# First x tiles in two loads, tile 0's key products ahead of tile 1's transposes, w1 in one load

## The chip, the cores and the metric

The kernel runs on one core of a Trainium2 chip. A core has TensorE (PE, with its weight loads listed apart as PEld), VectorE (DVE), ScalarE (ACT), GpSimd (POOL) and SyncE (SP), which here only issues DMAs. Each engine takes its instructions in order and waits on semaphores of the others. DMA transfers run on 16 DMA engines that all queues share. The metric is the device time of one execution in microseconds; before, the median of 4 runs is 178.98 us (178.72 to 179.65).

## The reference

x is [2048, 512] in bf16. A linear attention with 32 heads of 16 and a gated MLP with 1376 hidden columns work on the same x, and a gate per token mixes them:

```
g   = sigmoid((x * gate_w).sum(-1))
q, k, v = split(x @ wqkv)                      # 32 heads of 16
phi(t) = where(t > 0, t + 1, exp(t)) + 1e-6
kv  = phi(k)^T v   per head;  z = sum over tokens of phi(k)
a   = (phi(q) kv) / (phi(q) z + 1e-6) @ wo
b   = (silu(x @ w1) * (x @ w3)) @ w2
out = g * a + (1 - g) * b
```

## The kernel before

Tokens are worked in 16 tiles of 128 (index `t`) and 4 blocks of 512 (`tb`). All weights are loaded once into SBUF and stay. x is held twice: `x_sb`, tokens on partitions, and `xT`, features on partitions in four chunks `kc`.

**Loads (lines 78 to 111).** All but one are issued by SP, in the order of the code; ACT issues the first half of `wk_sb` (line 83). The first load brings x tiles 0 and 1 in one transfer, `x_first`: partition p gets rows 2p and 2p+1, 2 KB in one piece, so that tile 0 holds the even rows of the first 256 and tile 1 the odd ones. Their results are stored by the same rule (`out_first`, line 376). `xT` of tiles 2 and 3 comes by a DMA transpose from memory (line 87), that of the blocks 1 to 3 by three more (line 91), between which x tiles 2 to 15 are loaded (line 96). Then come wq, the remainder columns `wr_sb` with the gate's weights, wv, halves of w1 and w3 in turn (lines 105 to 107), wo, w2.

**The front (lines 153 to 181, 382 to 391).** TensorE's order is the order of the code (a manual schedule). It begins with nine matmuls on constants that nothing uses, `emit_warm` (line 165): six of 512 columns, three of 128. Then `xT` of tiles 0 and 1 is made by TensorE: `emit_xT(t)` does four 128x128 transposes into two PSUM buffers; VectorE copies the first two chunks to `xT` (line 179), ScalarE the other two (line 181). Then come the key products `emit_k_mm(k_ps, t, kc)` (line 184), 128x512 each, of tiles 0 to 3. Their first eight are in the order (kc, t) = (0,0), (1,0), (0,1), (1,1), (2,0), (3,0), and then chunks 2 and 3 of tile 1. Products of chunks 0 and 1 read the half of `wk_sb` that ACT loads, those of chunks 2 and 3 the half that SP loads (line 84). `emit_k_phi` (lines 138 to 148) turns a finished k into phi(k): exp on ScalarE (140), two operations on VectorE (142, 145), and a running sum on GpSimd.

**The rest.** For t from 4 on, `emit_xp` (line 204: x^T phi(k), in four PSUM banks through all tiles) of an earlier tile and `emit_k(t)` alternate. After that come q of block 0, the remainder columns, z, the product with wv, and W = kv wo folded. Then for each block the MLP's chunks `emit_ffn` (gate products line 312, up products line 320) and the output tiles `emit_out` (lines 353 to 362), with the next block's q between them. The last output tile is stored in three parts.

Of the kernel before, what the change touches and what calls it, by code (L numbers as in the profile page):

```python
# [17 lines left out]
def kernel(  # L18
# [13 lines left out]
    P = nc.NUM_PARTITIONS  # L32
# [7 lines left out]
    TB = 512  # L40
# [4 lines left out]
    FM = FC * P  # L45
# [3 lines left out]
    x2d = A_x.flatten_outer_dims()  # L49
    out2d = out.flatten_outer_dims()  # L50
# [11 lines left out]
    x_sb = consts.tile([P, NT, D], BF16, name="x_sb")  # L62
# [4 lines left out]
    w1_sb = consts.tile([P, KC, FM], BF16, name="w1_sb")  # L67
# [7 lines left out]
    w1_r = B_w1.rearrange("(kc d) f -> d kc f", d=P)  # L75
    w3_r = B_w3.rearrange("(kc d) f -> d kc f", d=P)
    x_r = x2d.rearrange("(t p) d -> p t d", p=P)
    dq = nc.sync
    TF = 2
    x_first = x2d[0 : TF * P, :].rearrange("(p j) d -> p j d", j=TF)  # L80
    out_first = out2d[0 : TF * P, :].rearrange("(p j) d -> j p d", j=TF)
    dq.dma_start(out=x_sb[:, 0:TF, :], in_=x_first)
    nc.scalar.dma_start(out=wk_sb[:, 0:2, :], in_=wqkv_r[:, 0:2, D : 2 * D])
    dq.dma_start(out=wk_sb[:, 2:4, :], in_=wqkv_r[:, 2:4, D : 2 * D])
    pre = consts.tile([1, 1], FP32, name="pre")
# [2 lines left out]
        out=xT[:, :, TF * P : TB], in_=x2d[TF * P : TB, :], transpose=True  # L88
    )
    for tb in range(1, NTB):  # L90
        dq.dma_start(
            out=xT[:, :, tb * TB : (tb + 1) * TB], in_=x2d[tb * TB : (tb + 1) * TB, :],
# [7 lines left out]
    with nc.allow_non_contiguous_dma(reason="one gate weight per partition and chunk"):  # L100
        dq.dma_start(
            out=wr_sb[:, :, 2 * FR : NR], in_=gate_w.rearrange("(kc d o) -> d kc o", d=P, o=1)
        )
    dq.dma_start(out=wv_sb[:], in_=wqkv_r[:, :, 2 * D : 3 * D])
    for fsl in (slice(0, FM // 2), slice(FM // 2, FM)):
        dq.dma_start(out=w1_sb[:, :, fsl], in_=w1_r[:, :, fsl])
        dq.dma_start(out=w3_sb[:, :, fsl], in_=w3_r[:, :, fsl])
    dq.dma_start(out=wo_sb[:], in_=A_wo.rearrange("(kc d) n -> d kc n", d=P))
    w2_r = B_w2[0:FM, :].rearrange("(fc f) d -> f fc d", f=P)
# [9 lines left out]
        out=bm, in_=bm, pattern=[[-Dh, HPC], [0, Dh]], compare_op=ALU.is_ge, fill=0.0,  # L119
# [3 lines left out]
        out=bm, in_=bm, pattern=[[Dh, HPC], [0, Dh]], compare_op=ALU.is_ge, fill=0.0,  # L123
# [34 lines left out]
    def emit_warm(*widths):  # L158
        warm = psX.tile([P, TB], FP32, tag="XP3", name="warm")
        for n in widths:  # L160
            nc.tensor.matmul(
                warm[:, 0:n], lhsT=warm_l, rhs=warm_r[:, 0:n], start=True, stop=True
            )

    emit_warm(TB, TB, TB, TB, TB, TB, P, P, P)

    st = {}

    def emit_xT(t):
        for h in range(2):  # L170
            xTp = psX.tile([P, 2, P], BF16, tag=f"XP{(2 * t + h) % 4}", name="xTp")
            for j in range(2):
                kc = 2 * h + j
                nc.tensor.transpose(  # L174
                    out=xTp[:, j, :], in_=x_sb[:, t, kc * P : (kc + 1) * P], identity=ident[:]
                )
            xT_t = xT[:, 2 * h : 2 * h + 2, t * P : (t + 1) * P]
            if h == 0:
                nc.vector.tensor_copy(out=xT_t, in_=xTp[:])  # L179
            else:  # L180
                nc.scalar.activation(out=xT_t, in_=xTp[:], func=ACT.Copy)

    def emit_k_mm(k_ps, t, kc):
        nc.tensor.matmul(  # L184
            k_ps[:], lhsT=xT[:, kc, t * P : (t + 1) * P], rhs=wk_sb[:, kc, :],
            start=(kc == 0), stop=(kc == KC - 1),
        )
# [148 lines left out]
    def emit_out(tb, tt):  # L336
        t = tb * TPB + tt
        tsl = slice(tt * P, (tt + 1) * P)

        if t < NT - 1:  # L340
            parts = [(0, D, True)]
        else:
            h, q7 = D // 2, 7 * D // 8
            parts = [(0, h, True), (h, q7, True), (q7, D, True)]
        if t < NT - 1:
            o_out = work.tile([P, D], BF16, tag="o_out", name="o_out")
        else:
            o_out = consts.tile([P, D], BF16, name="o_last")
        lo = 0
        for i, (a, b, store) in enumerate(parts):  # L350
            o_ps = psX.tile([P, b - a], FP32, tag=f"XP{2 + (tt + i) % 2}", name="o_ps")
            for c in range(KC):
                nc.tensor.matmul(  # L353
                    o_ps[:], lhsT=st[tb, "pqT"][:, c, tsl], rhs=W_sb[:, c, a:b],
                    start=(c == 0), stop=False,
                )
            nc.tensor.matmul(  # L357
                o_ps[:], lhsT=st[tb, "hTr"][:, tsl], rhs=w2r_sb[:, a:b],
                start=False, stop=False,
            )  # L360
            for fc in range(FC):
                nc.tensor.matmul(  # L362
                    o_ps[:], lhsT=st[tb, "hT"][:, fc, tsl], rhs=w2_sb[:, fc, a:b],
                    start=False, stop=(fc == FC - 1),
                )
            if i < 2:
                nc.scalar.activation(  # L367
                    out=o_out[:, a:b], in_=o_ps[:], func=ACT.Copy, scale=omg[:, t : t + 1]
                )
            else:  # L370
                nc.vector.tensor_scalar(
                    out=o_out[:, a:b], in0=o_ps[:], scalar1=omg[:, t : t + 1], scalar2=None,
                    op0=ALU.mult,
                )
            if store:
                rows = out_first[t] if t < TF else out2d[t * P : (t + 1) * P, :]
                eng = nc.scalar if i == 1 else nc.sync
                eng.dma_start(out=rows[:, lo:b], in_=o_out[:, lo:b])
                lo = b


    k0 = [psM.tile([P, D], FP32, tag="mm", name=f"k0_{t}") for t in range(TPB)]
    emit_xT(0)
    emit_xT(1)
    for kc, t in ((0, 0), (1, 0), (0, 1), (1, 1), (2, 0), (3, 0)):
        emit_k_mm(k0[t], t, kc)
    emit_k_phi(k0[0], 0)
    for t in range(1, TPB):
# [15 lines left out]
    with tc.manual_schedule(engines={ENG.DVE}):  # L404
# [18 lines left out]
        for dc in range(KC):  # L423
# [9 lines left out]
            out=z_sb[:].rearrange("p (b f) -> p b f", f=Q),  # L433
            in_=z_col[:, :, None].to_broadcast([P, NB, Q]),
        )
        kvT_ps = psX.tile([P, KC, P], FP32, tag="XP0", name="kvT_ps")
        for c in range(KC):
# [7 lines left out]
            out=kvT_sb[:], in0=kvT_ps[:],  # L445
# [22 lines left out]
    for tb in range(NTB):  # L468
        for fc in range(FC if tb == 0 else 0, FC):
            emit_ffn(tb, fc)  # L470
        nx = tb + 1
        for tt in range(TPB):
            if nx < NTB:
                emit_q(nx, tt, psX, "XP0")
                if tt % 2 == 0:
                    emit_rem(nx, tt // 2, psX, "XP1")
                    if tt == 2:
                        emit_omg(nx)
            emit_out(tb, tt)
            if nx < NTB:  # L480
                emit_den(nx, tt)
        if nx < NTB:
            emit_norm(nx)
# [30 lines left out]
```

## Time and profile before

| | |
|---|---|
| median of 4 runs | 178.98 us (178.72 to 179.65) |
| the profiled execution's own time | 178.82 us |
| its span, first to last instruction | 177.1 us |
| TensorE busy | 172.4 us, 97% |
| VectorE busy | 118.6 us, 67% |
| ScalarE, GpSimd busy | 65.4 and 63.9 us |
| DMA moved | 15.14 MB, mean 85 GB/s |

A row of the groups or of the timeline gives the line of the kernel, the engine, the operation and its tiles (out<-in). In the timeline the first two columns are start and length in us; the bracket at the end is idle time before it and what ended that. In the chain of waits the columns are start, length and what the time was spent in. Matmuls are pipelined, so a row of one matmul (379 ns) is longer than the step to the next. PEld rows mark when a matmul's weights are loaded, which is when its wait for data shows.

### The profile page before, as it was taken

The page shows a single profiled execution, that of the slowest core. Times are in us where ns is not written, and L with a number is a line of the kernel's source. Part 1 is how long each engine was busy: PE and PEld are TensorE (multiplying, and loading weights), DVE is VectorE, ACT ScalarE, POOL GpSimd, SP SyncE. Part 2 cuts the span into 40 slices and gives each one's busy share as a digit, 9 for nine tenths or more (in the row PEclk, how much of TensorE's full clock was granted, in tenths as well). Part 3 has the DMA queues.
Part 4 walks back from the last instruction along what each step waited for, and adds up shares of the span by engine and source line. Part 5 has one row for each costly group of instructions (what it writes and reads, how often), then busy time and mean ns, then how long its engine had stood idle before and what let it go on. Part 6 is the DMA issues. An engine that isn't in the chain of part 4 may idle for free.

```text
span 177.1 us, 2457 instructions
## 1 busy us (share of the span) xinstructions
PE 172.4 (97%) x867; PEld 83.4 (47%) x883; DVE 118.6 (67%) x204; ACT 65.4 (37%) x123; POOL 63.9 (36%) x80
## 2 busy tenths in 40 slices
PE   7999999999999999999999999999999999999993
PEld 3444444474445454444454544444545444444463
DVE  0586858899999637597876466978754668776000
ACT  3624224465433333334244333233434323241221
POOL 6197655789062323272003232710032328000000
PEclk9999999999999999999999999999999999999999
DMA  5999989941013011123000101230002022200012
GB/s 171 233 288 222 256 291 364 352 145 28 9 30 89 7 41 37 37 59 89 0 4 7 48 26 43 73 71 6 0 7 67 7 70 59 59 0 0 30 38 54
DMA packets 30380, 15.14 MB, mean 85 GB/s; under 512 B 20928, under 2 KB 30240, under 8 KB 30368
## 3 DMA queue, kind: packets, MB, share of 16 engines
q1 hardware_dynamic: 29952, 14.67, 30.5%
q10 hardware_dynamic: 416, 0.31, 0.5%
q8 instruction: 7, 0.11, 0.3%
q14 instruction: 5, 0.04, 0.1%
HBM read 8.42 MB, written 2.10 MB: 59 GB/s over the span
## 4 chain that ended last, share of the span: by engine, by line
PE 96%; DMA 2%; issue 1%; DVE 0%
PE o_ps L362 19%; PE gate_ps L312 19%; PE up_ps L320 19%; PE o_ps L353 8%; PE XP L204 8%; PE q_ps L217 8%; PE k_ps L184 6%; PE r_ps L241 3%; PE k L184 2%; PE o_ps L357 2%; DMA x_sb<-in_A_x_dram 2%; PE kvT_ps L440 1%; PE W_ps L458 0%; DVE xT L179 0%; PE xTp L174 0%
## 5 line engine op out<-in xcount | busy, mean ns | idle before, releaser
L312 PE MATMUL gate_ps<-xT,w_sb 128*128 128x512 bf16 x157 | 40.7, 379 | 0.2
L320 PE MATMUL up_ps<-xT,w_sb 128*128 128x512 bf16 x157 | 40.7, 379 | 0.2
L225 POOL TENSOR_TENSOR qz<-pq,z_sb 128x512 f32<-128x512 bf16 x16 | 18.5, 1164 | 58.0 <-DVE pq L145 58.0
L325 ACT ACTIVATE th<-gate_ps 128x512 bf16<-128x512 f32 x40 | 23.9, 597 | 39.0 <-PE gate_ps L312 37.5
L362 PE MATMUL o_ps<-w_sb,hT 128*128 128x512 bf16 (+3 forms) x177 | 37.3, 355 | 0.2
L327 DVE SCALAR_TENSOR_TENSOR gs<-th,gate_ps 128x512 bf16<-128x512 bf16 x40 | 27.3, 682 | 5.4 <-ACT th L325 5.1
L332 DVE TENSOR_TENSOR hT<-up_ps,gs 128x512 bf16<-128x512 f32 x40 | 27.6, 691 | 3.8
L142 DVE TENSOR_SCALAR phi_m<-phi_e 128x512 bf16<-128x512 bf16 x32 | 13.6, 425 | 21.1 <-ACT phi_e L140 20.9
L362 PEld LDWEIGHTS <-hT 128*128 128x128 bf16 x180 | 16.9, 98 | 17.8
L320 PEld LDWEIGHTS <-w_sb 128*128 128x128 bf16 x160 | 15.7, 98 | 18.9
L312 PEld LDWEIGHTS <-w_sb 128*128 128x128 bf16 x160 | 15.6, 98 | 18.6
L292 POOL TENSOR_TENSOR pqn<-pq,rden 128x512 bf16<-128x512 bf16 x16 | 16.6, 1057 | 15.1 <-DVE rden L285 13.1
L367 ACT ACTIVATE o_out<-o_ps,omg 128x512 bf16<-128x512 f32 x15 | 10.3, 688 | 28.9 <-PE o_ps L362 28.9
L194 POOL TENSOR_TENSOR pks<-pks,pk_sb 128x512 f32<-128x512 f32 x15 | 17.5, 1170 | 7.3 <-DVE pk_sb L145 6.7
L353 PE MATMUL o_ps<-W_sb,pqT 128*128 128x512 bf16 (+3 forms) x70 | 16.7, 355 | 0.1
L204 PE MATMUL XP<-pk_sb,x_sb 128*128 128x512 bf16 x62 | 16.2, 379 | 0.1
L228 DVE TENSOR_REDUCE den<-qz 128x32 f32<-128x512 f32 x16 | 10.9, 684 | 7.9 <-POOL qz L225 7.9
L217 PE MATMUL q_ps<-wq_sb,xT 128*128 128x512 bf16 x61 | 16.1, 379 | 0.1
L140 ACT ACTIVATE phi_e<-k_ps 128x512 bf16<-128x512 f32 x12 | 7.2, 597 | 14.4 <-PE k_ps L184 14.4
L140 ACT ACTIVATE phi_e<-q_ps 128x512 bf16<-128x512 f32 x16 | 9.6, 597 | 7.8 <-PE q_ps L217 6.7
L184 PE MATMUL k_ps<-wk_sb,xT 128*128 128x512 bf16 x48 | 12.3, 379 | 0.0
L145 DVE SCALAR_TENSOR_TENSOR pq<-q_ps,phi_m 128x512 bf16<-128x512 f32 x16 | 11.1, 691 | 0.5
(60 smaller groups left out, 118.4 us busy)
## 6 DMA issues: line engine op xcount, KB each, us to landing
w_sb<-in_B_w_dram SPq DMA_DIRECT2D x4, 640.0 KB, 6.8
out_dram<-o_out SPq DMA_DIRECT2D x15, 128.0 KB, 1.9
w_sb<-in_B_w_dram SPq DMA_DIRECT2D x1, 1280.0 KB, 12.3
x_sb<-in_A_x_dram SPq DMA_DIRECT2D x2, 512.0 KB, 5.2
x_sb<-in_A_x_dram SPq DMA_DIRECT2D x1, 768.0 KB, 5.1
wq_sb<-in_A_wqkv_dram SPq DMA_DIRECT2D x1, 512.0 KB, 6.5
wv_sb<-in_A_wqkv_dram SPq DMA_DIRECT2D x1, 512.0 KB, 6.7
wo_sb<-in_A_wo_dram SPq DMA_DIRECT2D x1, 512.0 KB, 9.5
```

The source lines that it names most:

```text
L184: nc.tensor.matmul(k_ps[:], lhsT=xT[:, kc, t * P : (t + 1) * P], rhs=wk_sb[:, kc, :], start=(kc == 0), stop=(kc == KC - 1),)
L194: nc.gpsimd.tensor_add(pks[:], pks[:], pk_sb[:, t, :])
L204: nc.tensor.matmul(XP_ps[dc][:], lhsT=x_sb[:, t, dc * P : (dc + 1) * P], rhs=pk_sb[:, t, :], start=(t == 0), stop=(t == NT - 1),)
L217: nc.tensor.matmul(q_ps[:], lhsT=xT[:, kc, ts_tok], rhs=wq_sb[:, kc, :], start=(kc == 0), stop=(kc == KC - 1),)
L225: nc.gpsimd.tensor_tensor(out=qz[:], in0=st[tb, "pq"][:, tt, :], in1=z_sb[:], op=ALU.mult)
L312: nc.tensor.matmul(gate_ps[:], lhsT=w1_sb[:, kc, fsl], rhs=xT[:, kc, tok_sl], start=(kc == 0), stop=(kc == KC - 1),)
L320: nc.tensor.matmul(up_ps[:], lhsT=w3_sb[:, kc, fsl], rhs=xT[:, kc, tok_sl], start=(kc == 0), stop=(kc == KC - 1),)
L325: nc.scalar.activation(out=th[:], in_=gate_ps[:], func=ACT.Tanh, scale=0.5)
L327: nc.vector.scalar_tensor_tensor(out=gs[:], in0=th[:], scalar=1.0, in1=gate_ps[:], op0=ALU.add, op1=ALU.mult)
L332: nc.vector.tensor_tensor(out=st[tb, "hT"][:, fc, :], in0=up_ps[:], in1=gs[:], op=ALU.mult)
L353: nc.tensor.matmul(o_ps[:], lhsT=st[tb, "pqT"][:, c, tsl], rhs=W_sb[:, c, a:b], start=(c == 0), stop=False,)
L362: nc.tensor.matmul(o_ps[:], lhsT=st[tb, "hT"][:, fc, tsl], rhs=w2_sb[:, fc, a:b], start=False, stop=(fc == FC - 1),)
```

## The change

The first two x tiles are loaded by one transfer each, in plain row order (partition p gets row p of the tile, 1 KB); their stores are in plain row order too. The warm-up has one 512-column matmul less. TensorE does tile 0's transposes, then tile 0's products of chunks 0 and 1, then tile 1's transposes, then the remaining products as before. w1's main columns come in one transfer of 1280 KB, ahead of the two halves of w3. On SP there is thus one issue more at the front and one less at the weights. The order on VectorE, ScalarE and GpSimd is as before.

```diff
     TF = 2
-    x_first = x2d[0 : TF * P, :].rearrange("(p j) d -> p j d", j=TF)
-    out_first = out2d[0 : TF * P, :].rearrange("(p j) d -> j p d", j=TF)
-    dq.dma_start(out=x_sb[:, 0:TF, :], in_=x_first)
+    for t in range(TF):
+        dq.dma_start(out=x_sb[:, t, :], in_=x_r[:, t, :])
...
     dq.dma_start(out=wv_sb[:], in_=wqkv_r[:, :, 2 * D : 3 * D])
+    dq.dma_start(out=w1_sb[:], in_=w1_r[:, :, 0:FM])
     for fsl in (slice(0, FM // 2), slice(FM // 2, FM)):
-        dq.dma_start(out=w1_sb[:, :, fsl], in_=w1_r[:, :, fsl])
         dq.dma_start(out=w3_sb[:, :, fsl], in_=w3_r[:, :, fsl])
...
-    emit_warm(TB, TB, TB, TB, TB, TB, P, P, P)
+    emit_warm(TB, TB, TB, TB, TB, P, P, P)
...
-                rows = out_first[t] if t < TF else out2d[t * P : (t + 1) * P, :]
+                rows = out2d[t * P : (t + 1) * P, :]
...
     emit_xT(0)
+    emit_k_mm(k0[0], 0, 0)
+    emit_k_mm(k0[0], 0, 1)
     emit_xT(1)
-    for kc, t in ((0, 0), (1, 0), (0, 1), (1, 1), (2, 0), (3, 0)):
+    for kc, t in ((0, 1), (1, 1), (2, 0), (3, 0)):
         emit_k_mm(k0[t], t, kc)
```

## The prediction

> **What bounds the kernel now.** I read the page's first part, then the chain that ended last, then the timeline of the first 16 us (the diff touches nothing later but one weight load), and last the landings of the loads.
>
> ```profile
> PE 172.4 (97%) x867; PEld 83.4 (47%) x883; DVE 118.6 (67%) x204; ACT 65.4 (37%) x123; POOL 63.9 (36%) x80
> ```
>
> TensorE works 172.4 of 177.1 us, so outside the front only work added to it or a hole in it can cost. The chain, cut to the first 12 us (start, us, what):
>
> ```profile
> 0.81 2.97 DMA x_sb<-in_A_x_dram
> 3.78 0.05 issue
> 3.83 0.30 PE xTp L174 x2
> 4.13 0.02 issue
> 4.15 0.30 DVE xT L179
> 4.45 0.05 issue
> 4.50 3.74 PE k L184 x16
> 8.24 0.86 PE XP L204 x4
> ```
>
> From 4.50 on it is TensorE alone to the end. So the change can move the time only by moving what TensorE does before about 8 us, or by opening a hole later. The timeline of that stretch (start, us, engine, line), first the weight loads of TensorE, one ahead of each matmul, then SP's DMA issues:
>
> ```profile
> 2.93 0.15 PEld L161 LDWEIGHTS <-const-bfloat16-1.0 128*128 128x128 bf16 x1 [0.28 <-issue]
> 3.36 0.21 PEld L161 LDWEIGHTS <-const-bfloat16-1.0 128*128 128x128 bf16 x2 [0.28 <-issue]
> 3.82 0.45 PEld L174 LDWEIGHTS <-x_sb 128*128 128x128 bf16 x8 [0.25 <-DMA x_sb<-in_A_x_dram]
> 4.50 1.41 PEld L184 LDWEIGHTS <-xT 128*128 128x128 bf16 x8 [0.22 <-DVE xT L179]
> 6.33 1.41 PEld L184 LDWEIGHTS <-xT 128*128 128x128 bf16 x8 [0.43 <-DMA xT<-in_A_x_dram]
> 7.86 0.74 PEld L204 LDWEIGHTS <-x_sb 128*128 128x128 bf16 x4
> ...
> 11.31 0.75 PEld L204 LDWEIGHTS <-x_sb 128*128 128x128 bf16 x4
> ```
>
> ```profile
> 0.81 0.40 SPq L82 DMA_DIRECT2D x_sb<-in_A_x_dram  x1
> 1.27 0.41 SPq L84 DMA_DIRECT2D wk_sb<-in_A_wqkv_dram  x1
> 1.73 1.32 SPq L87 DMA_TRANSPOSE xT<-in_A_x_dram  x1
> ```
>
> Three things are to be seen. A 512-wide warm-up matmul takes 0.43 us (2.93 to 3.36), a 512-wide key product 0.216 (chain: four in 0.86): the array ran at half pace until about 3.5 us and at full pace from the first transposes on, eight of which take 0.45. The first key product waited for VectorE's copy (0.22), 0.67 us after the transposes began (3.83 to 4.50). And tile 2's products wait at 6.33 for the DMA transpose of line 87. Two more landings matter, ACT's half of wk and the x tiles 2 to 7 (which the products at 11.31 read):
>
> ```profile
> L83 ACTq DMA_DIRECT2D wk_sb<-in_A_wqkv_dram x1: 449/449/449, 0.8 to 0.8; - x1
> ...
> DMA to landing us min/median/max: 3.6/3.6/3.6
> ```
>
> ```profile
> x_sb<-in_A_x_dram SPq DMA_DIRECT2D x1, 768.0 KB, 5.1
> ```
>
> wk's first half lands at 0.80 + 3.6 = 4.40, just before the 4.50 at which it is used. The x tiles land at 6.01 (issue, SP's timeline) + 5.1 = 11.11 for a use at 11.31.
>
> **The change, step by step.**
>
> *Two x loads.* SP's issues stand 0.46 us apart (0.81, 1.27, 1.73), so one more puts each later one 0.46 later: wk's second half, the line 87 transpose, the next transpose, x tiles 2 to 7. Tile 0's 128 KB lands no sooner than the 128 KB stores of o_out do (1.9 us after issue in the page's list: 2.71) and no later than the 256 KB load (3.78). I take 3.2, nearer the load, since both share the engines with wk; tile 1 at about 3.8. The Trainium skill, "DMA: Bandwidth & Descriptors" (Anatomy of one DMA), gives a fixed 2.0 us plus bytes over 436 GB/s and its rules ask for large transfers; estimated from it, tile 0 lands 2.3 us after issue, at 3.1, and a second load pays the fixed part again. By that page the 256 KB load would take 2.6 us; the trace has 2.97, and the sum would not move, as wk comes later than either.
>
> *One warm-up matmul less.* The warm-up ends 0.43 earlier, at 3.30 instead of 3.73. Tile 0's four transposes then start at max(3.30, 3.2) = 3.30.
>
> *Tile 0's products first.* Its copy is done 0.67 after 3.30, at 3.97, or at about 4.1 if the array is still at half pace. But the products need wk's first half: 4.40. Bounds: 3.97 if wk lands early, 5.27 if x tile 1 pushes it back to where wk's second half landed (1.27 + 4.0); I take 4.40, the same load on the same queue with the same bytes ahead. The two products end at 4.40 + 2 x 0.216 = 4.83. Now tile 1's four transposes (0.45 / 2 = 0.22), its VectorE copy and its ScalarE copy are behind them. The next product in TensorE's order is tile 1's first, behind the same 0.67: 4.83 + 0.67 = 5.50, with TensorE idle from 5.05 to 5.50. Before, that copy ran beside the eight transposes. On VectorE and ScalarE nothing stands before these copies; behind them are tile 0's exp and phi, which start after 6.5 anyway. The other six products take 6 x 0.216 = 1.30: TensorE is ready for tile 2 at 6.80, where before it was ready at 4.50 + 8 x 0.216 = 6.23 and began at 6.33. Net +0.47.
>
> *The DMA transposes behind.* Line 87's would land at 6.33 + 0.46 = 6.79 if its issue sets the landing, about 6.4 if the DMA engines do (their share is full from 3.5 to 7.5 us). Both are at or under 6.80, so it adds nothing. x tiles 2 to 7 land at 11.11 + 0.46 = 11.57 at worst; use moves to 11.31 + 0.47 = 11.78. It hides, but it is a floor: were the products not late, these would be, by 11.57 - 11.31 = 0.26.
>
> *Tile 0's phi.* It starts 0.41 after tile 0's last product does (5.59, exp at 6.00). That product moves by about 0.55 to 6.14, so pk of tile 0 is ready at 7.65 + 0.55 = 8.20; its use moves from 7.86 to 8.33. Hidden by 0.13; without that cover at most 0.1.
>
> *w1 in one load.* One issue of 0.55 less, so SP is level again from there. w1 then lands where w1's and w3's first halves did together: second issue 22.67 + 6.1 (landings by line) = 28.8, w3's first half at 30.6 (23.22 + 7.4), its second still at about 32.5 (23.77 + 8.7). The first gate product is at 37.93, the first up product at 38.79. Eight us cover it: zero, and it would take a landing later by that much to cost. The loads behind, wo and w2, are issued no later.
>
> *Stores of tiles 0 and 1* write rows of 1 KB either way, over 100 us before the end: zero.
>
> Sum: from tile 2 on TensorE has no room to make it up, so 178.82 (the profiled execution's own time, span 177.1) + 0.47 = 179.29. The median of the runs shown, 178.98, is 0.16 above that execution.
>
> **Rivals.**
>
> *The clock stays at half pace longer.* In the trace full pace came after about 2.6 us of unbroken work (0.84 to about 3.5). After, unbroken work ends at 3.30 and TensorE idles from 3.5 to 4.4 and 5.05 to 5.50. If full pace now needs 2.6 us of unbroken work from tile 1's products on, these run at 0.43: two of tile 0's (+0.42), the transposes (+0.22) and six more until the grant (+1.27): +1.9, so 181.2. It decides once two products beyond 3.5 us are at half pace. For it: the half-pace rows above, 0.43 us less warm-up, and the times before, which spread from 178.72 to 179.65. Against it: what was busy before 3.5 us stays busy until 3.30, so the grant at 3.5 should come as before. The Trainium skill, "TensorE: Matmul & The Clock Gate" (Part 1), has a free-running window of 3.4 us instead: one that ended near 3.5 was 77% busy before and would be 72% after, so by it the sum keeps +0.47 if 72% passes and loses a window or more if it does not. Its Part 4 says transposes do not count as busy; nothing in this trace shows either.
>
> *The front is absorbed (not slower).* If wk lands by 4.0, tile 0's products start at 3.97 and TensorE is ready for tile 2 at 6.37. If moreover the DMA engines' work and not the issue sets the landings, both floors go: +0.05, so 178.9. For it: DMA share over 1 until 7.5. Against: wk landed at 4.40 with nothing said of why it would be sooner. A gain over 0.5% has no mechanism: even here tile 2 begins no earlier than 6.33.
>
> *wk pushed back by tile 1's load.* k starts at 5.27: +0.87 more, 180.2. For it: both share 16 engines; against: the same bytes as before.
>
> **How the numbers follow.** As sketched (+0.2 to +0.85, 179.0 to 179.7): 0.60. Clock late (180.3 to 181.5): 0.20. Absorbed (178.7 to 179.0): 0.12. wk late: 0.06. Something faster that I do not see: 0.02. Half a per cent, 0.9 us, is about what a measurement of this kernel can tell from no change; the likeliest lies inside it. Slower: the clock, wk and 0.06 for a tail of the likeliest, 0.32; faster 0.04, the unseen and as much for the absorbed case measured low; within, 0.64. Range 178.9 to 180.9 leaves out the upper end of the clock's case and half of the absorbed one; the likeliest alone has 179.0 to 179.7.
>
> **What would show it.** In the changed profile: tile 0's transposes at 3.3 us; its first product at about 4.4, released by the wk load and not by the copy; a hole of about 0.45 at 5.05 ended by VectorE's copy of tile 1; tile 2 at about 6.8; all later TensorE work 0.47 later; w1 and w3 waited for by no one. I am wrong if the first product starts by 4.0, if products beyond 3.5 us stand 0.43 apart, or if a load is waited for after 8 us.

## The result, and the profile after

The changed kernel takes 179.45 us (median of 44 runs, 178.71 to 181.51); before, taken beside it, 179.19 us (63 runs, 178.48 to 179.73). Compared side by side the ratio is 1.0023, with a 95% interval of 1.0013 to 1.0033: 179.19 x 0.0023 = 0.41 us slower (the medians over all times, which come from several sets, stand 0.26 apart), inside the half per cent that the prediction called no change, close to its +0.47. (Ratios leave out times more than 1.5% above the fastest of the same kernel, here 181.44 and 181.51; medians and highest times keep them.) The number was right, in part by luck: the path to it was not the predicted one, and two profiles of the changed kernel show why.

The first of them comes from an execution of 180.13 us with a span of 178.3 (before 177.1). Its chain of waits, first 12 us (start, us, what):

```profile
3.49 0.41 PE xTp L173 x2
...
4.27 1.03 PE k L183 x2
5.30 0.23 PE xTp L173 x2
...
5.56 0.30 DVE xT L178
...
5.91 3.76 PE k L183 x14
9.66 0.86 PE XP L203 x4
```

The new order is there as written: tile 0's two products, tile 1's transposes, VectorE's copy, and the rest. But all of it is long. The weight loads of the same execution (start, us, then what the wait ended with):

```profile
5.90 0.13 PEld L183 LDWEIGHTS <-xT 128*128 128x128 bf16 x2 [0.44 <-DVE xT L178]
6.30 0.15 PEld L183 LDWEIGHTS <-xT 128*128 128x128 bf16 x1 [0.28 <-ACT xT L180]
6.73 0.15 PEld L183 LDWEIGHTS <-xT 128*128 128x128 bf16 x1 [0.28 <-issue]
7.13 2.04 PEld L183 LDWEIGHTS <-xT 128*128 128x128 bf16 x10 [0.25 <-issue]
9.29 0.74 PEld L203 LDWEIGHTS <-x_sb 128*128 128x128 bf16 x4
```

Up to 7.13 the products stand 0.43 us apart, after it 0.2: TensorE ran at half pace until about 7.1 us, where in the profile before it had full pace by 3.8. (The clock row of the page shows full clock in both; the trace's own record of the full clock begins at 7.08 us here and at 3.47 before. Moments of full pace are taken from these records and from the steps of the products.) That is the rival called "the clock stays at half pace longer". It is not the usual execution, though: the time of this one, 180.13, is higher than all but four of the 44. The same kernel profiled again, an execution of 179.53 us:

```profile
3.31 0.34 PEld L173 LDWEIGHTS <-x_sb 128*128 128x128 bf16 x4
4.10 0.11 PEld L183 LDWEIGHTS <-xT 128*128 128x128 bf16 x2 [0.44 <-DVE xT L178]
4.33 0.42 PEld L173 LDWEIGHTS <-x_sb 128*128 128x128 bf16 x4
5.20 0.33 PEld L183 LDWEIGHTS <-xT 128*128 128x128 bf16 x3 [0.45 <-DVE xT L178]
6.30 0.53 PEld L183 LDWEIGHTS <-xT 128*128 128x128 bf16 x3 [0.77 <-issue]
7.30 1.41 PEld L183 LDWEIGHTS <-xT 128*128 128x128 bf16 x8 [0.47 <-DMA xT<-in_A_x_dram]
8.82 0.74 PEld L203 LDWEIGHTS <-x_sb 128*128 128x128 bf16 x4
```

Here full pace came before the first product. The hole before tile 1's products is there with the predicted 0.45 us (row 5.20). It is not what ends last: TensorE idles again before 6.30 and before 7.30. The bracket of such a row is idle time of the weight loads. TensorE's own, with its products counted at 0.216 us, is less: two products from 5.21 end at 5.65, so it stood 0.65 us before 6.30, and 0.14 before 7.30. What it waited for is in the chain of that execution, and in the landings of line 86 (line 87 before), the DMA transpose of tiles 2 and 3:

```profile
1.73 4.53 DMA wk_sb<-in_A_wqkv_dram
6.25 0.04 issue
6.30 2.90 PE k L183 x12
```

```profile
L86 SPq DMA_TRANSPOSE xT<-in_A_x_dram x1: 1561/1561/1561, 2.2 to 2.2; - x1
...
DMA to landing us min/median/max: 5.1/5.1/5.1
```

wk's second half landed at 6.26 instead of 1.27 + 4.0 = 5.27, the transpose at 2.20 + 5.1 = 7.30 instead of 6.33. Each was issued 0.46 to 0.47 later and landed 1.0 later. The 4.0 is from the profile before (line 84):

```profile
L84 SPq DMA_DIRECT2D wk_sb<-in_A_wqkv_dram x1: 410/410/410, 1.3 to 1.3; - x1
...
DMA to landing us min/median/max: 4.0/4.0/4.0
```

One row serves as a mark below: the weight load of the first x^T phi(k) product (L203 here, L204 before), at 7.86 before, 9.29 and 8.82 after, so +1.43 and +0.96. In both executions every later weight load up to the last output tiles is late by that same amount, to within 0.01 us. The whole difference arises in the first 9 us. The spans differ by 0.25 less, since the very last store landed 1.7 us after its issue in the profile before and after 1.4 in both of these (the 64 KB store ahead of it: 2.7, 1.9 and 2.2).

### The profile page after: what moved, and what is told of

Its sections match the earlier page's. It is cut to its first block, busy times and chain, and to the rows that moved or that the text cites. A ratio compares the mean times of both kernels' runs of the same rounds, so it can differ in the third digit from the quotient of the medians.

```text
span 178.3 us, 2455 instructions
## 1 busy us (share of the span) xinstructions
PE 173.6 (97%) x866; PEld 83.8 (47%) x882; DVE 118.7 (67%) x204; ACT 65.6 (37%) x123; POOL 63.7 (36%) x80
## 4 chain that ended last, share of the span: by engine, by line
PE 97%; issue 1%; DVE 0%
PE o_ps L361 19%; PE gate_ps L311 19%; PE up_ps L319 19%; PE o_ps L352 8%; PE XP L203 8%; PE q_ps L216 8%; PE k_ps L183 6%; PE r_ps L240 3%; PE k L183 3%; PE o_ps L356 2%; PE warm L160 1%; PE kvT_ps L441 1%; PE W_ps L459 0%; PE xTp L173 0%; DVE xT L178 0%
## 5 line engine op out<-in xcount | busy, mean ns | idle before, releaser
L203 PE MATMUL XP<-pk_sb,x_sb 128*128 128x512 bf16 x62 | 16.2, 379 | 0.1
```

Of the source, the lines that this page charges most:

```text
L203: nc.tensor.matmul(XP_ps[dc][:], lhsT=x_sb[:, t, dc * P : (dc + 1) * P], rhs=pk_sb[:, t, :], start=(t == 0), stop=(t == NT - 1),)
```

## The experiments

Three theories stand in the expectations. By the order theory, the one of the prediction (called front theory in the first round), the hole before tile 1's products sets the time. By the clock theory the moment of full pace does. The load theory came out of the first round's profiles: SP's extra issue sets the time, through wk's second half and line 87. Every kernel was timed in five rounds beside the kernel before. The intervals of nearly all slower versions overlap: the ratios tell a version from the kernel before, but not these versions from one another, so what separates the theories is mainly one profile each.

| kernel | ratio to before, 95% interval | times | highest | mark in its profile |
|---|---|---|---|---|
| changed kernel again | 1.0033 (1.0007 to 1.0058) | 12 | 181.49 | 8.82 |
| order only | 1.0037 (1.0010 to 1.0063) | 12 | 182.11 | 8.54 |
| loads only | 1.0025 (1.0010 to 1.0041) | 12 | 180.19 | 8.65 |
| five warm-up matmuls only | 1.0004 (0.9985 to 1.0023) | 12 | 180.00 | 8.08 |
| w1 only | 1.0002 (0.9987 to 1.0018) | 12 | 179.61 | 8.23 |
| changed, old order | 1.0050 (1.0021 to 1.0079) | 12 | 181.97 | 10.48 |
| changed, breaks filled | 1.0027 (1.0012 to 1.0041) | 12 | 179.79 | 8.70 |
| loads only, wk by ACT | 1.0029 (1.0013 to 1.0045) | 12 | 180.40 | 7.92 |
| before, wk by ACT | 1.0037 (1.0019 to 1.0055) | 12 | 180.12 | 7.93 |
| changed, wk by ACT | 1.0014 (0.9997 to 1.0032) | 12 | 179.87 | 7.96 |
| changed, six warm-up matmuls | 1.0043 (1.0019 to 1.0067) | 9 | 181.11 | 9.27 |
| before, no warm-up | 1.0096 (1.0076 to 1.0116) | 4 | 180.79 | 9.34 |

### The changed kernel again

No edit.

> The changed kernel once more, for a second profile and a spread of times. Front theory (the hole before tile 1's products): tile 1's first product 1.64 us after tile 0's first at half pace or 1.10 at full pace, median 0.3 to 0.5 us above before whatever the clock. Clock theory (full pace is granted at a moment that moves from execution to execution, and the change makes it late more often): the lowest time within 0.3 us of the lowest of before, the highest 1.5 us or more above the highest of before, and in a profile in which full pace comes by 3.7 us the span is at most 0.3 us longer than the 177.1 of before.

Measured: 12 times from 178.91 to 181.49, two above 180.6. The second profile shown above is of this run; it had full pace before 4.1 (record: 3.87) and a span of 177.8, 0.7 longer than before. The clock theory had allowed 0.3 for the span and for the lowest time, which lies 0.37 above the lowest of before; its 1.5 for the highest times is reached (1.63). So a late clock can explain the highest times, of which none was profiled, and something else the usual ones. Tile 1's first product came 1.10 us behind tile 0's, as the order theory said for full pace.

### Order only

```diff
     emit_xT(0)
+    emit_k_mm(k0[0], 0, 0)
+    emit_k_mm(k0[0], 0, 1)
     emit_xT(1)
-    for kc, t in ((0, 0), (1, 0), (0, 1), (1, 1), (2, 0), (3, 0)):
+    for kc, t in ((0, 1), (1, 1), (2, 0), (3, 0)):
```

> Before, with only tile 0's products of chunks 0 and 1 moved ahead of tile 1's transposes. Front theory: tile 0's first product at 4.50 as before, tile 1's copy behind it, a hole of 0.45 us, tile 2 at 6.8 to 6.9, median +0.45 to +0.55 us. Clock theory: the hole is after the warm-up of 3.73 us, so full pace comes as often by 3.5 as before; median +0.5 with no tail above 180.5. Rival that the order is hidden behind line 87's landing at 6.33: +0.1 or less.

Measured: median 179.75 against 179.01. The weight loads:

```profile
4.61 0.11 PEld L184 LDWEIGHTS <-xT 128*128 128x128 bf16 x2 [0.45 <-DVE xT L179]
4.84 0.43 PEld L174 LDWEIGHTS <-x_sb 128*128 128x128 bf16 x4
5.72 2.70 PEld L184 LDWEIGHTS <-xT 128*128 128x128 bf16 x14 [0.45 <-DVE xT L179]
8.54 0.75 PEld L204 LDWEIGHTS <-x_sb 128*128 128x128 bf16 x4
```

With the loads of before the hole is the last wait: fourteen products follow it without a break. It costs what the prediction worked out: the mark is 0.68 later, of which 0.11 is a later start of tile 0's first product (4.61 for 4.50), and the prediction's steps from a start at 4.50 give 0.57 (4.50 + 1.10 + 1.30 = 6.90 for 6.33). The rival that line 87's landing hides it is out. The clause on the tail was wrong: two of 12 times, 181.65 and 182.11, lie above 180.5.

### Loads only

```diff
-    x_first = x2d[0 : TF * P, :].rearrange("(p j) d -> p j d", j=TF)
-    out_first = out2d[0 : TF * P, :].rearrange("(p j) d -> j p d", j=TF)
-    dq.dma_start(out=x_sb[:, 0:TF, :], in_=x_first)
+    for t in range(TF):
+        dq.dma_start(out=x_sb[:, t, :], in_=x_r[:, t, :])
...
-                rows = out_first[t] if t < TF else out2d[t * P : (t + 1) * P, :]
+                rows = out2d[t * P : (t + 1) * P, :]
```

> Before, with only the two x loads (and plain rows of their stores). Front theory: wk's second half, line 87 and the rest are issued 0.46 us later; wk's first half at 4.1 to 4.4, the eight products from 4.2 to 4.5, tile 2 at 6.4 if the DMA engines set line 87's landing, 6.8 if its issue does, 7.2 if it lands 5.0 us after issue as in the changed kernel's profile: median +0.1, +0.47 or +0.87 us. Clock theory: nothing, as TensorE is as busy as before until 3.7; 0 us.

Measured: median 179.61 against 179.01, with TensorE's order of before.

```profile
4.47 0.23 PEld L173 LDWEIGHTS <-x_sb 128*128 128x128 bf16 x4 [0.43 <-DMA x_sb<-in_A_x_dram]
4.65 0.15 PEld L183 LDWEIGHTS <-xT 128*128 128x128 bf16 x2
5.14 0.33 PEld L183 LDWEIGHTS <-xT 128*128 128x128 bf16 x3 [0.34 <-DVE xT L178]
6.12 0.53 PEld L183 LDWEIGHTS <-xT 128*128 128x128 bf16 x3 [0.65 <-issue]
7.13 1.41 PEld L183 LDWEIGHTS <-xT 128*128 128x128 bf16 x8 [0.48 <-DMA xT<-in_A_x_dram]
8.65 0.75 PEld L203 LDWEIGHTS <-x_sb 128*128 128x128 bf16 x4
...
12.47 0.55 PEld L203 LDWEIGHTS <-x_sb 128*128 128x128 bf16 x4 [0.48 <-DMA x_sb<-in_A_x_dram]
```

Tile 1 of x is waited for until 4.47, wk's second half until 6.12 (1.73 + 4.3), line 86 until 7.13 (2.20 + 4.9). The highest of the three values expected for tile 2, 7.2, was the right one. The x tiles 2 to 7 came late too, at 12.43 for a use at 12.10, and cost 0.17 us more. So each part costs about the whole by itself (ratios 1.0037 and 1.0025), and together they cost no more (1.0023 and 1.0033): in the profiles the hole of the order lies inside the waits for the loads.

### Five warm-up matmuls only

```diff
-    emit_warm(TB, TB, TB, TB, TB, TB, P, P, P)
+    emit_warm(TB, TB, TB, TB, TB, P, P, P)
```

> Before, with only one 512-column warm-up matmul less. TensorE then idles from 3.30 to 3.82. Front theory: nothing waits for the warm-up, 0 us. Clock theory: full pace comes later in some executions; median +0.1 to +0.6 us, the highest time above 180.2, and in the profile the step between the first key products is 0.43 us if full pace has not come by 3.7.

Measured: no difference beyond the interval, highest time 180.00. The expected rise of up to 0.6 us is not shown. In the profile, the transposes ran at half pace (eight in 0.77) and the products from 5.00 on at full pace (record: 4.66):

```profile
3.80 0.77 PEld L174 LDWEIGHTS <-x_sb 128*128 128x128 bf16 x8 [0.61 <-DMA x_sb<-in_A_x_dram]
...
5.00 1.04 PEld L184 LDWEIGHTS <-xT 128*128 128x128 bf16 x6 [0.25 <-DVE xT L179]
6.55 1.41 PEld L184 LDWEIGHTS <-xT 128*128 128x128 bf16 x8 [0.50 <-DMA xT<-in_A_x_dram]
```

### The changed kernel with the old order

The changed kernel with `emit_xT(0)`, `emit_xT(1)` and the eight products as before:

```diff
     emit_xT(0)
-    emit_k_mm(k0[0], 0, 0)
-    emit_k_mm(k0[0], 0, 1)
     emit_xT(1)
-    for kc, t in ((0, 1), (1, 1), (2, 0), (3, 0)):
+    for kc, t in ((0, 0), (1, 0), (0, 1), (1, 1), (2, 0), (3, 0)):
```

> The changed kernel with TensorE's old order (both tiles' transposes, then the eight products); two loads, five warm-up matmuls and w1 in one load stay. Order theory (the hole before tile 1's products sets the time): back to the kernel before, median within 0.15 us of it, tile 2 at 6.3 to 6.5. Load theory (SP's extra issue sets it: wk's second half lands at 6.1 to 6.3, line 87 at 7.1 to 7.3): tile 2 at 7.1 to 7.3 all the same, median +0.4 to +0.7 us. Either way no time above 180.6 if the tail of the changed kernel comes from the breaks in TensorE's work that the new order makes.

Measured: median 179.59 against 178.89, not back to before (the eight times below 180 have a median of 179.42), so the order theory falls for the changed kernel. The statement on the tail fell too: four of 12 times lie between 180.89 and 181.97, and the execution profiled, 181.19 us, is one of them:

```profile
3.50 0.34 PEld L173 LDWEIGHTS <-x_sb 128*128 128x128 bf16 x4 [0.32 <-DMA x_sb<-in_A_x_dram]
4.60 0.35 PEld L173 LDWEIGHTS <-x_sb 128*128 128x128 bf16 x4 [0.75 <-DMA x_sb<-in_A_x_dram]
...
9.27 0.15 PEld L183 LDWEIGHTS <-xT 128*128 128x128 bf16 x1 [0.28 <-issue]
9.62 0.75 PEld L183 LDWEIGHTS <-xT 128*128 128x128 bf16 x4 [0.19 <-issue]
10.48 0.53 PEld L203 LDWEIGHTS <-x_sb 128*128 128x128 bf16 x3
```

Half pace until about 9.5 us. TensorE waits here for tile 1's load, about 0.7 us from the transposes of tile 0 on. It shows also that the loads are not always late: wk's second half landed at 1.73 + 3.6 = 5.33 and line 86 at 2.20 + 4.1 = 6.3. What kept the usual times of this version high no profile shows.

### The breaks filled

```diff
     emit_xT(0)
+    emit_warm(P, P, P)
     emit_k_mm(k0[0], 0, 0)
     emit_k_mm(k0[0], 0, 1)
     emit_xT(1)
+    emit_warm(P, P, P, tag="XP0")
```

(`emit_warm` gets the PSUM buffer's tag as an argument.)

> The changed kernel with three 128-column matmuls on constants behind tile 0's transposes and three behind tile 1's, in the two breaks. If the tail (times of 180.7 to 181.5) comes from a clock grant that is missed because TensorE idles there, the tail goes: highest time under 180.4, and full pace in the profile by 4.7 us. If the breaks do not matter for the clock, about one time in nine is still above 180.6. The median stays at +0.3 to +0.6 us either way, since the loads and the copies are where they were; if the added matmuls are in the way, up to 0.3 more.

Measured: no time above 179.79, median 179.47 against 178.89, as high as without the filling. Full pace from 3.9 us in the profile (record: 3.89), wk's second half waited for until 6.15, line 86 until 7.17. The tail, the times above 180.6, is not seen here, as a clock that depends on TensorE's work would have it; against 6 of 56 times above 180.6 in the unfilled kernel, 0 of 12 is weak evidence. The median stays, so filling repairs nothing of the loads.

### wk's second half issued by ACT: loads only

```diff
-    dq.dma_start(out=wk_sb[:, 2:4, :], in_=wqkv_r[:, 2:4, D : 2 * D])
+    nc.scalar.dma_start(out=wk_sb[:, 2:4, :], in_=wqkv_r[:, 2:4, D : 2 * D])
```

on top of the two loads.

> Before with the two x loads alone, and wk's second half issued by ACT behind its first half, so that SP issues line 87 at 1.73 as before. Load theory: with SP's extra issue made good, line 87 lands at 6.3 to 6.5, wk's second half by 5.6; tile 2 at 6.3 to 6.5 and the median back to within 0.15 us of before. If instead the two small transfers themselves (256 pieces of 1 KB for 128 of 2 KB) are the cause, line 87 lands at 6.8 or later and the median stays at +0.3 to +0.6.

Measured in the profile: line 86, again issued at 1.73, landed 4.4 later, and nothing was waited for after the copy:

```profile
5.09 2.70 PEld L183 LDWEIGHTS <-xT 128*128 128x128 bf16 x14 [0.33 <-DVE xT L178]
7.92 0.74 PEld L203 LDWEIGHTS <-x_sb 128*128 128x128 bf16 x4
```

The mark is back to within 0.06 of before. So the small pieces by themselves do not make the landings late; in this profile and the one with the same edit on the changed kernel they are in time with SP's issue made good. As two of the six profiles with the extra issue have them nearly in time as well, the extra issue is the likely cause and not a proven one. Nor is the time back: 1.0029, where the load theory had said within 0.15 us. The execution profiled was the fastest of the 12 (179.00), and what the others lost it cannot show.

### wk's second half issued by ACT: before

The same edit on the kernel before.

> Before with only wk's second half issued by ACT, so that SP issues line 87 at 1.27 instead of 1.73 and all behind it 0.46 earlier. If SP's issue sets line 87's landing, tile 2 waits no more and starts at 6.23 instead of 6.33: median -0.1 to -0.3 us, a version faster than both. If the work of the DMA engines sets it, or wk's second half now lands after 5.4, 0 to +0.3.

Measured: slower, 1.0037, so no version that beats both. In the profile the x load landed at 3.9 instead of 3.78, and line 87, issued 0.46 earlier, at 1.27 + 5.1 = 6.4 instead of 6.33. Issuing it earlier than before brings nothing. That execution took 178.84, the second lowest of the 12, and the cause of the higher ones is not shown.

### wk's second half issued by ACT: the changed kernel

The same edit on the changed kernel.

> The changed kernel with wk's second half issued by ACT, so that SP issues line 87 at 1.73 as before. Load theory: wk's second half lands at 5.3 to 5.4 and line 87 at 6.3 to 6.5, so what is left is the order's own cost: tile 1's first product 1.10 us after tile 0's first at full pace (4.1 + 1.1 = 5.2), tile 2 at 6.5 instead of 7.2 to 7.3, and in a profile with full pace by 4.1 us the shift against before at 11 us is 0.1 to 0.3 us instead of 0.96. Median +0.1 to +0.4 us. Order theory: shift and median as in the changed kernel, +0.4 to +0.6.

Measured: 1.0014 (0.9997 to 1.0032), no time above 179.87.

```profile
4.03 0.11 PEld L183 LDWEIGHTS <-xT 128*128 128x128 bf16 x2 [0.45 <-DVE xT L178]
4.40 0.29 PEld L173 LDWEIGHTS <-x_sb 128*128 128x128 bf16 x4 [0.25 <-DMA x_sb<-in_A_x_dram]
5.13 2.70 PEld L183 LDWEIGHTS <-xT 128*128 128x128 bf16 x14 [0.45 <-DVE xT L178]
7.96 0.75 PEld L203 LDWEIGHTS <-x_sb 128*128 128x128 bf16 x4
```

Both waits at 6.3 and 7.3 are gone and the hole is the last wait. The mark is 0.10 behind before: tile 0's products start 0.47 earlier than the 4.50 of before, which nearly pays for the hole. The intervals of this kernel and of the changed one overlap, so the times do not prove it; the two profiles with early full pace (3.87 and 3.49) show it for one execution each.

### Six warm-up matmuls in the changed kernel

The line of `emit_warm` as before.

> The changed kernel with the sixth 512-column warm-up matmul put back: the transposes start at 3.75 instead of 3.3 to 3.5 and tile 0's products at 4.4 to 4.5. If the tail comes from TensorE being too little at work in the 3.4 us before a possible grant, it goes or halves (one time in twelve or none above 180.6), and full pace comes by 4.3 us or between 4.3 and 7. Load theory: the median stays at +0.4 to +0.6 us, since wk's second half and line 87 still land at 6.1 and 7.2, after everything that starts 0.3 later. Order theory: 0.3 more, +0.7 to +0.9.

Measured: 1.0043, which is 0.77 us, with medians 0.42 apart; one of nine times lies above 180.6. The median is as the load theory said, the ratio as the order theory, so this run does not separate them, and the tail is neither clearly gone nor clearly there. The execution profiled (180.13) had half pace until about 6.9 us:

```profile
6.90 2.26 PEld L183 LDWEIGHTS <-xT 128*128 128x128 bf16 x11 [0.23 <-issue]
9.27 0.75 PEld L203 LDWEIGHTS <-x_sb 128*128 128x128 bf16 x4
```

### w1 only

```diff
+    dq.dma_start(out=w1_sb[:], in_=w1_r[:, :, 0:FM])
     for fsl in (slice(0, FM // 2), slice(FM // 2, FM)):
-        dq.dma_start(out=w1_sb[:, :, fsl], in_=w1_r[:, :, fsl])
```

> Before with only w1 in one load. Both theories: zero, median within 0.15 us of before; w1 lands by 30, w3's first half by 31.5, uses at 37.9 and 38.8, and no wait for either.

Measured: 1.0002 (0.9987 to 1.0018), zero. w1 landed at 21.9 + 7.0 = 28.9, the two halves of w3 between 30.8 and 32.5. Its front is that of before, and its profile is of use for another reason: full pace came at about 5.4 us (record: 5.31), and the mark is 0.37 later than in the profile before. From 5.42 on the products follow one another without a break; the bracket at 6.58 is of the weight loads alone.

```profile
5.43 0.96 PEld L184 LDWEIGHTS <-xT 128*128 128x128 bf16 x5 [0.17 <-issue]
6.58 1.53 PEld L184 LDWEIGHTS <-xT 128*128 128x128 bf16 x8 [0.19 <-DMA xT<-in_A_x_dram]
8.23 0.74 PEld L204 LDWEIGHTS <-x_sb 128*128 128x128 bf16 x4
```

### No warm-up

```diff
-    emit_warm(TB, TB, TB, TB, TB, TB, P, P, P)
```

> Before without any warm-up matmul, to price a late grant. TensorE begins with the transposes at 3.8. Clock theory: full pace comes between 6 and 10 us, all key products until then take 0.43 us instead of 0.216; median +1.2 to +2 us and no time below +0.7. If full pace came with the first dense work within 1 us, less than +0.5.

Measured: 1.0096 (1.0076 to 1.0116), 1.7 us, with four times from 180.45 to 180.79. The products stood 0.43 apart until 7.54. A late clock is thus worth 1 to 2 us here (record: 7.67), the size of the changed kernel's tail.

## Why the prediction was right, and where it was not

**The number.** +0.47 was predicted against one execution's own time, +0.41 is the ratio in us. The time lies in the range, and within half a per cent of before. That the two agree so closely is in part luck: in the profile the step that the sum consists of, the hole, is covered by two landings that the sum has at nothing. The prediction's own signs say so too. Tile 0's first product was released by the copy and not by wk, tile 2 began at 7.30 and not at 6.8, later work came 0.96 and not 0.47 later, and products beyond 3.5 us stood 0.43 apart in one of the two profiles.

**The hole of the order: right in size, wrong in its part.** Tile 1's first product came 1.10 us after tile 0's (4.10 to 5.20), as worked out (4.40 to 5.50), with 0.45 of idling. Order only shows that it costs this by itself. In the changed kernel it does not end last.

**wk's first half: 4.40 was wrong.** It landed at 0.80 + 3.1 = 3.9 and 0.80 + 3.3 = 4.1, so tile 0's products were released by VectorE's copy (4.10, 4.27). The prediction had this only as the lower bound. The 0.3 us so won were lost again in the wait for wk's second half.

**wk's second half: the term that was missing.** The step on the two loads names it among the issues that move by 0.46 and then never holds it against its use. By that rule it would land at 5.73, for a use at 5.93; it landed at 6.0 to 6.3 in four of the six profiles with SP's extra issue (5.3 and 5.6 in the others), and at full pace TensorE idled 0.65, 0.53 and 0.38 us before it (changed kernel again, loads only, breaks filled).

**Line 87: "6.4 to 6.79, it adds nothing" was wrong.** It landed at 7.2, 7.3, 7.1 and 7.1 (changed kernel twice, loads only, breaks filled), 0.3 to 0.5 above the upper bound, and at 6.8 and 6.3 in the other two: the bound shifted the landing by the issue alone, and the transpose came by about twice that. Its issue on SP was longer too, 1.55 to 1.78 us instead of 1.32 in the four late ones, and 1.49 and 1.32 in the other two. With it tile 2 starts at 7.30 for 6.80. What was taken as a hidden step was the one that ends last, if only by 0.14: after wk's second half TensorE was ready at 7.16. Tile 1 of x, too, landed at 4.3 to 4.6 in all profiles with two loads, not at 3.8.

**Why +0.96 in the second profile and +0.41 by the ratio.** Of the 0.96 the last store gives back 0.25, and the two executions' own times differ by 0.71. The one before lies 0.37 below its kernel's median and this one 0.08 above, which leaves the 0.26 between the medians. So it is the usual execution of before that is slower than the profiled one. The kernel before also loses in executions with late full pace: w1 only, whose front is the same, shows a mark 0.37 later with full pace at 5.4. In the changed kernel products at half pace between 4 and 7 us cost less, as TensorE waits for loads there anyway. And the loads are not always late (old order: 6.3). That these two make up the difference is argued, not shown; there is no trace of the other timed executions.

**The clock rival: real, at about its price.** It was priced at 181.2 with a chance of 0.20. Four of 44 times lie between 180.8 and 181.5, two more of 12 in the second sample, and profiled executions with half pace until 7.1 and 9.5 us took 180.13 and 181.19. So it can have made the tail; the median stayed high in breaks filled, where no time lies in the tail. Full pace came anywhere from 3.49 to 9.53 us in kernels whose first 3 us are alike. The Trainium skill, "TensorE: Matmul & The Clock Gate" (Part 1), describes a free-running window of 3.4 us. The 13 traces with a clock record agree: in each the full clock lasts 50 or 51 times 3.413 us. Windows of that length, laid back from its start, give an estimate of what decides it (products, warm-up matmuls and transposes counted by their width at the pace that held). TensorE was at work for 76.8% or more of each window that ended in full pace, and for 75.6% or less of each that did not: 75.6% in the window that ended at 3.67 in the first profile of the changed kernel, 72.1% in the one that ended at 6.11 in the old order. Without the transposes the groups overlap (58.7% enough, 70.4% not), so here they seem to count, unlike what the prediction takes from Part 4. By this estimate the kernel does not set when a window ends, but the breaks in TensorE's work decide whether one passes, and each of these two executions lost a window to them. That the unprofiled high times come so is not shown.

**The smaller steps.** w1: zero, as said; in the changed kernel's first profile it landed at 20.39 + 8.2 = 28.6 for a use at 39.30. Phi and the stores: no wait seen. The x tiles 2 to 7 landed at 12.0 in both profiles of the changed kernel, not at "11.57 at worst", and were hidden only because their use had moved too, to 12.28 in the second; in loads only they were waited for. The formula that the prediction takes from "DMA: Bandwidth & Descriptors" (Anatomy of one DMA) is by that section's heading one for DMAs that GpSimd issues. SP's tile 0 landed 2.6 and 2.5 us after issue, for the 2.3 estimated from it. The Trainium skill, "DMA: Bandwidth & Descriptors" (Rules for kernel authors), asks for few large transfers. That pointed the right way; what cost the time in the profiles, though, was not the small loads' own landing but that of the others behind them in SP's queue.

**Open.** Why loads only and before, with wk issued by ACT, have ratios of 1.0029 and 1.0037 while their profiles stand within 0.07 us of before; both profiles are of executions at the low end of their times. Why the transfers behind SP's extra issue came late in four profiles and not in two is open as well.

## What to carry to other kernels

When a load is split at the head of a queue, hold every later load of that queue against its own use, and bound its landing by more than the added issue time: here 0.46 us of issue became 0.8 to 1.0 us of landing in four of six profiles. When two waits lie side by side, undo each alone and both: each part cost about the whole here, and undoing the more visible one gained nothing that the times show. A profile is one execution: where times of one kernel spread over 1 us, read in it at which pace the matmuls run before comparing spans.

## What was not expected of the hardware

- Full pace of TensorE came at moments from 3.5 to 9.5 us in these profiles, and that in kernels with the same first 3 us (changed kernel: 3.87 and 7.08).
- With a second small load ahead of them, the transfers of the same queue landed 0.8 to 1.0 us later in four of six profiles. ACT's load beside them landed 0.2 to 0.4 earlier (3.9 to 4.2 for 4.4) in all six, and also in the two where wk's second half was ACT's and nothing came late (4.0 and 3.9).
- In loads only the shift of 0.79 at the mark had become 0.96 behind the wait at 12.47, and 0.36 us more was lost near 40 us. The chain goes there through VectorE, in whose queue z's transpose and the gate's factor stand ahead of the first gate chunk:

```profile
39.90 0.71 DVE z_sb L431
40.61 0.58 DVE kvT_sb L443
41.19 0.96 DVE om L271
...
42.17 0.18 DVE omg L275
42.35 0.59 DVE gs L326
```

The kernel without warm-up lost 0.40 at the same place. The others did not.
